# K of batches 2 to 7 by a casting DMA and DMA transposes, in an attention and SwiGLU kernel

## The chip, the core and the metric

One core of a Trainium2 chip runs the whole program. Its engines work side by side, each through its own queue of instructions in order, and wait for each other through semaphores: PE (TensorE; the profile lists its weight loads apart, as PEld), DVE (VectorE), ACT (ScalarE), POOL (GpSimd) and SP (SyncE, which here only issues DMAs). Sixteen DMA engines move data for all queues. The metric is the device time of the program in microseconds (us). Three runs of the kernel before gave 383.66, 384.03 and 384.58 us; their median is 384.03.

## What is computed

Causal attention over 8 batches of 8 heads, 576 tokens and 64 values per head, with a decay from the running sums of `s`, followed by RMS norm and a gated feed-forward network (FFN) over the 8 x 576 = 4608 tokens of width 512:

```python
scores = scale * np.matmul(q, k.transpose(0, 1, 3, 2))
cum = np.cumsum(np.maximum(s, 0.0), axis=-1)
bias = -(cum[:, :, :, None] - cum[:, :, None, :])
scores = np.where(causal, -1000000000.0, scores + np.minimum(bias, 0.0))
attn = np.exp(scores - max); attn = attn / sum
x = matmul(attn, v)                       # heads side by side: 4608 x 512
xn = x / sqrt(mean(x * x) + 1e-6) * rms_g
g = xn @ w_gate; silu = g / (1 + exp(-g))
out = (silu * (xn @ w_val)) @ w_out       # 512 -> 1536 -> 512
```

Inputs and output are float32; the kernel's matmuls run in bfloat16 (bf16). A second, general path in the program is taken only where a test on the data fails; it isn't taken here.

## The kernel before

**Two kinds of work on one queue.** The FFN goes over nine chunks of 512 tokens (`ffn`, L622). For each chunk PE makes twelve pairs of groups of four 128x512 matmuls (L632 for the gate, L641 for the value) and then four output blocks of twelve matmuls (L654). That is 36 groups of four. After each group `step` (L566) is called once: one *slot*. In a slot a scheduler written in the kernel may put a piece of attention of a coming batch behind the FFN group. So the order on every engine is fixed when the program is built; the scheduler counts slots and knows no times. The conditions are written as "so many slots after" (`ready`), and if something is late on the chip, the engine that needs it waits with everything behind it.

**The pieces of attention.** The 576 tokens of a batch are five blocks of 128 (the last of 64). Scores are computed transposed, keys in rows.

- *Loads* (`load_kq`, L122): K and Q of a batch in float32 by DMAs of the ACT queue, four tokens per row, into `kq32`, 1024 KB and a tail of 128 KB each. V (`load_v`, L162) by blocks with DMAs from POOL that cast to bf16, 128 KB each as written.
- *Casts*: POOL casts K (`cast`, L140) and Q (`cast_x`, L148) to bf16 in `kqn`, which has two halves, for even and odd batches; five casts each per batch.
- *Check* (`check_mag`, `check_max`): DVE takes the greatest magnitude of K and of Q.
- *Transposes of Q* (`kq_dma`, L152) for batches 2 to 7 (`XB` is 2): five DMA transposes on SP into `kqTx`, the blocked view of `kqT`, four of them from 32 rows and the last from 64.
- *Transposes of K* for all batches, and of Q for batches 0 and 1: the T step (`t_step`, L169) of a pair of heads makes four PE matmuls against the identity into a PSUM bank, and ACT (for K) copies the result into `kqTn`, the view of `kqT` by heads. A tail step (`tail_step`, L183) does the last 64 tokens with four matmuls for K. The bank has the tag T, which the second AV step of a block uses too (L281).
- *S step* (`s_step`, L214) of batch b, key block kb and half g of the heads, written S(b,kb,g): scores of a key block against its own query block and the next, four matmuls of 64x256 (L236), then eight exps on ACT (L260) and a mask on POOL (L269).
- *AV step* (`av_step`, L278): eight matmuls with V (L286, L292), division on DVE, squares on ACT, then `al_all` on POOL.
- *xnT*: DVE scales the rows (L324), and a DMA transpose on SP (L334) puts them into `xnT`, which the FFN reads.

**Queues.** SP carries, in order, the transposes of Q, those for xnT and the output stores (L661). POOL carries casts, V loads, masks and `al_all`. `x_seq` holds the waiting transposes of Q, which are issued at least two slots apart; `t_seq` the T steps, and `can_t` keeps these two or three slots apart for batches 2 and later; `can_s` (L509) lets an S step go when its Q transposes were issued five slots before and its T steps three. `casts(b + 2)` is queued by the tail step of batch b.

Of the kernel before, what the change touches and what calls it, by code (L numbers as in the profile page):

```python
# [26 lines left out]
def kernel(  # L27
# [12 lines left out]
    nc = tc.nc  # L40
# [6 lines left out]
    NSC = 5  # L47
# [94 lines left out]
    def cast_x(eng, b, w, hp):  # L142
# [6 lines left out]
        else:  # L149
            cast(eng, b, w, 4, 5)  # L150

    def kq_dma(b, w, c):  # L152

        if c < 4:
            src = kqn[32 * c:32 * c + 32, b % 2, w, 0:4].rearrange("p r h d -> p (r h d)")
            dst = kqTx[:, b % 2, w, c].rearrange("d h (r p) -> d (h r) p", r=4)
        else:
            src = kqn[0:64, b % 2, w, 4].rearrange("p h d -> p (h d)")
            dst = kqTx[:, b % 2, w, 4, :, 0:64]
        nc.sync.dma_start_transpose(out=dst, in_=src)  # L160
# [21 lines left out]

    def tail_step(b):  # L183
        pT = psT()
        nw = 2 if b < XB else 1
        for w in range(nw):
            for hp in range(HP):
                i = w * HP + hp
                nc.tensor.matmul(
                    pT[:, i, :], lhsT=kqn[:, b % 2, w, 4, 2 * hp:2 * hp + 2, :],  # L190
                    rhs=ident_bf, is_transpose=True, start=(i == 0), stop=(i == nw * HP - 1))
        dst, src = kqTn[:, b % 2, 0, :, 512:576], pT[:, 0:HP, 0:64]
        if b == 0:
            nc.vector.tensor_copy(out=dst, in_=src)
        else:
            nc.scalar.activation(out=dst, in_=src, func=AF.Copy)
        if nw == 2:
            nc.vector.tensor_copy(out=kqTn[:, b % 2, 1, :, 512:576], in_=pT[:, HP:8, 0:64])
# [15 lines left out]
    def s_step(b, kb, g, pair=None):  # L214

        p = b % 2
        N = (256, 256, 256, 192, 64)[kb]
        W = 64 if kb == 4 else 256
        nj = 4 if kb == 4 else 2
        e = take_slot((b, kb, g), 2 if kb in (0, 1, 2, 3) else 2)  # L220
        if pair is None:
            ps = psS()
            pair = (ps[:, 0, :], ps[:, 1, :])
        heads = []
        for j in range(nj):
            hp = (0 if kb == 4 else 2 * g) + j
            for par in (0, 1):
                rs = slice(par * 64, par * 64 + 64)
                kT = kqTn[rs, p, 0, hp, kb * 128:kb * 128 + 128]
                if b < XB:  # L230
                    qT = kqTn[rs, p, 1, hp, kb * 128:kb * 128 + N]
                    M = N
                else:
                    qT = kqTx[rs, p, 1, kb, hp, 0:64] if kb == 4 else kqTx[rs, p, 1, kb:kb + 2, hp, :]
                    M = W
                nc.tensor.matmul(  # L236
                    pair[par][:, j * W:j * W + M], lhsT=kT, rhs=qT,
                    start=(j == 0), stop=(j == nj - 1))
# [36 lines left out]
        second.mask = mask  # L275
        return second
# [82 lines left out]
    def check_max(i):  # L359
# [12 lines left out]
    s_seq.sort(key=lambda x: (1, 0, x[2], x[1]) if x[0] == 1 and x[1] < 2 else (x[0], x[1], x[2], 0))  # L372
    av_seq = [(b, qb, g) for b in range(B) for qb in range(NSC) for g in (0, 1)]
    xt_seq = [(b, qb) for b in range(B) for qb in range(NSC)]
    t_seq = [(b, hp, w) for b in range(B) for hp in list(range(HP)) + ["tail"]
             for w in (0, 1) if w == 0 or (hp != "tail" and b < XB)]
    t_seq.sort(key=lambda x: (x[0], 9, 0, 0) if x[1] == "tail" else
               (x[0], x[1] // 2, x[2], x[1]) if x[0] == 1 else (x[0], x[2], x[1], 0))
# [4 lines left out]
    def at(*key):  # L383
        return done.get(key, 10 ** 6)

    def ready(lag, *key):
        return at(*key) + lag <= slot[0]
# [13 lines left out]
        t = slot[0] + lag  # L401
        queue.extend((lambda: slot[0] >= t and phase() < 24, f) for f in fns)

    def check(b, ws=(1, 0)):
        dve_side.extend((lambda: (phase() >= 25 if b > 1 else slot[0] % 2
                                  and chunk[0] == b), f) for w in ws for f in (
            lambda w=w: check_mag(b, w), lambda: check_max(0), lambda: check_max(1),
            lambda w=w: done.__setitem__(("check", b, w), slot[0])))

    def phase():  # L410

        return slot[0] - first[0]
# [14 lines left out]
    def casts(b):  # L427


        def over(w):  # L430
            done["cast", b, w] = slot[0]
            if b + 1 < B:
                loads(b + 1, w, early, 4)
            if w == 1:
                x_seq.extend((b, 1, c) for c in range(NSC))
            else:
                done["cast", b] = slot[0]
                check(b)
        fns = [(1, lambda r=r: cast_x(nc.gpsimd, b, 1, r)) for r in range(NSC)]
        fns += [(1, lambda: over(1))]  # L440
        fns += [(0, lambda r=r: cast(nc.gpsimd, b, 0, r, r + 1)) for r in range(NSC)]
        pool_side.extend((lambda w=w: ready(7, "raw", b, w) and ready(0, "check", b - 2, w)
                          and (b < XB + 2 or ready(4, "X", b - 2, 1, 4)), f)
                         for w, f in fns + [(0, lambda: over(0))])

    def after_tail(b):
        if b + 2 < B:
# [49 lines left out]
    def can_t():  # L497
        if not t_seq:
            return False
        b, hp, w = t_seq[0]  # L500
        if b >= XB and at(*(("XT", 1, 3) if b == 2 else ("AV", b - 1, (2, 1, 0, 0, 0)[b - 3], 1))) > slot[0]:
            return False
        if b >= XB and av_seq[0][2] == 1 and can_av(True):
            return False
        if slot[0] - last["T"] < (1 if b < XB else 2 if b < 4 else 3) or slot[0] - last["AVT"] < 3:
            return False
        return (ready(2, "cast", b) or ready(2, "cast", b, w)) and (b < 2 or ready(1, "S", b - 2, 4, 0))

    def can_s():  # L509
        if not s_seq or not slot_free():  # L510
            return False
        b, kb, g = s_seq[0]
        if b == 1 and (phase() < 24 and phase() % 2 == 0 or kb == 4 and at("AV", 1, 3, 1) > slot[0]):
            return False
        due = SLOTS * ((b * S + kb * 128) // DM) - (26 if b == 1 else 18 if b < 4 else 14)
        if slot[0] - last["S"] < (4 if slot[0] < due - 24 else 3 if slot[0] < due else 2):
            return False
        if b >= XB:
            return (all(ready(5, "X", b, 1, c) for c in (kb, min(kb + 1, 4))) and (
                ready(3, "T", b) if kb >= 3 else  # L520
                all(ready(3, "T", b, hp, 0) for hp in (2 * g, 2 * g + 1))))
        if kb >= 3 and not ready(3, "T", b):
            return False
        if kb == 4:
            return True
        return all(ready(3, "T", b, 2 * g + j, w) for j in (0, 1) for w in (0, 1))
# [39 lines left out]
    def step(bare=False):  # L566
# [15 lines left out]
        run_side(act_side)  # L582
        if not moved and x_seq and slot[0] - last["X"] >= 2:
            b, w, c = x_seq[0]
            if ready(2, "cast", b, 1) and ready(1, "S", b - 2, 4, 0):
                x_seq.pop(0)
                kq_dma(b, w, c)
                done["X", b, w, c] = last["X"] = slot[0]
        bare = bare or chunk[0] == 0 and 30 <= phase() <= 33
        if slot[0] % 2 and not bare:  # L590
            run_side(v_side)
# [12 lines left out]
        if can_av():  # L604
            do_av(av_seq.pop(0))
            n += 1
        if n < 2 and can_t():
            do_t(t_seq.pop(0))

    def need(c):  # L610
# [124 lines left out]
    with tc.manual_schedule():  # L735
# [127 lines left out]
            lambda: load_v(1, 3), lambda: load_v(1, 4)])  # L863

        loads(2, 1, later, 14)
        loads(2, 0, later, 18)
        check(0, (0,))
        check(1)
        casts(2)
# [193 lines left out]
```

## Time and profile before

The profiled execution spans 383.2 us from its first to its last instruction; the granted TensorE clock is 0.995 of full speed on average.

| What | us | Where it is read |
|---|---|---|
| median of the runs | 384.03 | the times |
| span of the profiled execution | 383.2 | head of the page |
| PE / DVE / ACT / POOL busy | 349.6 / 286.1 / 247.4 / 172.7 | part 1 of the page |
| first FFN matmul of chunk 0, 1, 2, 8 | 31.5, 76.6, 115.6, 345.0 | weight loads of L632 |
| POOL casts of L140 (of K, and of tails) | 46, 32.6 in all | part 5 |
| V loads, issue on POOL | 40, 35.4 in all | part 5 |
| V load, issue to landing | 3.4 / 4.8 / 19.0 | min, median, max of tile v_sb |
| xnT transpose, issue to landing | 2.9 | median, part 6 of the page by DMA |
| DMA queues' time, of 16 engines | 30.5%, 26.6%, 15.3% | q0 (POOL), q1 (SP), q10 (ACT) |

How to read it: a busy share is an average over the whole span. PE's matmuls overlap in the array, so a matmul's own duration (about 0.38 us for 512 columns) is longer than the distance between two of them (about 0.21 us); what an instruction costs PE's queue is seen from the start of the next group. The time of a DMA's packets contains what they wait for each other, so the shares of the queues can add up to more than the engines have.

### The profile page before, as it was taken

To read this page: it belongs to the slowest core of one execution; us is meant where nothing else is said; L and a number is where in the kernel's file an instruction comes from. 1 tells how busy PE (TensorE), PEld (TensorE's weight loads), DVE (VectorE), ACT (ScalarE), POOL (GpSimd) and SP (SyncE) were. 2 spreads that over 40 slices of the span, in tenths; PEclk is the share of its full clock that TensorE was granted. 3 is DMA by queue.
4 is the path that set the end of the run, shared out by engine and by line. 5 is a ranking of instruction groups with operands and counts; after the bars stand their busy time and mean duration, and the time that the engine had idled before them with its cause. 6 is when DMAs were issued, how large, how long until landed. Compare 5 with 4: busy or idle time off the path is not lost. (4 is left out here: it accounts for less than half of the span.)

```text
span 383.2 us, 7015 instructions
## 1 busy us (share of the span) xinstructions
PE 349.6 (91%) x2391; PEld 165.5 (43%) x2436; DVE 286.1 (75%) x525; ACT 247.4 (65%) x646; POOL 172.7 (45%) x277
## 2 busy tenths in 40 slices
PE   1767999899999999999989999999999999999992
PEld 1443544444444444444434444444444444444441
DVE  6768988499888879987988977984388539837720
ACT  3777787457886687768678757776986774323311
POOL 5866725956774496619734764362223220000000
PEclk9999999999999999999999999999999999999997
DMA  7999999999998896796559083981200221020011
GB/s 232 183 229 232 141 221 179 149 200 196 131 187 214 172 173 98 197 201 51 78 186 225 16 89 92 122 63 42 98 15 9 55 98 21 3 83 28 2 56 60
DMA packets 103292, 46.24 MB, mean 121 GB/s; under 512 B 78481, under 2 KB 98449, under 8 KB 103249
## 3 DMA queue, kind: packets, MB, share of 16 engines
q0 software_dynamic: 41168, 9.44, 30.5%
q1 hardware_dynamic: 43184, 21.97, 26.6%
q10 hardware_dynamic: 18896, 14.30, 15.3%
q8 instruction: 21, 0.34, 0.4%
q14 instruction: 23, 0.18, 0.2%
HBM read 38.16 MB, written 9.44 MB: 124 GB/s over the span
## 5 line engine op out<-in xcount | busy, mean ns | idle before, releaser
L260 ACT ACTIVATE E<-psS,biasK 128x256 bf16<-128x256 f32 (+3 forms) x352 | 114.3, 427 | 8.7 <-PE psS L236 7.6
L641 PE MATMUL psF<-xnT,wv_sb 128*128 128x512 bf16 x417 | 110.0, 380 | 1.0 <-DVE Ht L637 0.2
L632 PE MATMUL psF<-xnT,wg_sb 128*128 128x512 bf16 x419 | 109.1, 379 | 1.8 <-ACT xnT L350 0.7
L654 PE MATMUL psF<-wout_sb,Ht 128*128 128x512 bf16 x416 | 100.8, 379 | 0.8 <-issue 0.2
L269 POOL TENSOR_SCALAR_AFFINE_SELECT E<-E 128x512 bf16<-128x512 bf16 x72 | 52.8, 733 | 94.8 <-ACT E L260 94.1
L635 ACT ACTIVATE T<-psF 128x512 f32<-128x512 f32 x108 | 64.5, 600 | 46.8 <-PE psF L632 40.1
L644 DVE SCALAR_TENSOR_TENSOR U<-T,psF 128x512 bf16<-128x512 f32 x108 | 73.7, 682 | 22.3 <-ACT T L635 22.1
L637 DVE TENSOR_TENSOR Ht<-U,psF 128x512 bf16<-128x512 bf16 x99 | 67.6, 683 | 7.1 <-PE psS L236 0.5
L632 PEld LDWEIGHTS <-wg_sb 128*128 128x128 bf16 x432 | 38.9, 97 | 42.8 <-issue 4.8
L654 PEld LDWEIGHTS <-Ht 128*128 128x128 bf16 x432 | 38.6, 98 | 42.8 <-issue 3.3
L641 PEld LDWEIGHTS <-wv_sb 128*128 128x128 bf16 x432 | 38.1, 98 | 43.0 <-issue 6.4
L324 DVE SCALAR_TENSOR_TENSOR xs_sb<-x_sb,al_all,g_row 128x512 bf16<-128x512 bf16 (+1 forms) x40 | 33.6, 842 | 16.0 <-POOL al_all L317 15.2
L307 ACT ACTIVATE xs_sb<-x_sb 128x512 bf16<-128x512 bf16 (+1 forms) x36 | 22.8, 637 | 32.5 <-DVE x_sb L301 31.8
L659 ACT ACTIVATE osb<-psF 128x512 f32<-128x512 f32 x36 | 21.7, 602 | 28.2 <-PE psF L654 20.2
L164 POOL DMA_DIRECT2D v_sb<-in_v_dram x40 | 35.4, 884 | 0.0
L140 POOL CAST kqn<-kq 128x512 bf16<-128x512 f32 (+1 forms) x46 | 32.6, 728 | 3.9 <-DMA kq<-in_k_dram 3.9
L361 DVE TENSOR_TENSOR acc<-acc,mag 128x1280 bf16<-128x1280 bf16 x32 | 32.4, 1034 | 0.3
L314 POOL TENSOR_SCALAR al_all<-ss_all 128x1 f32<-128x1 f32 (+1 forms) x40 | 10.9, 272 | 45.2 <-ACT xs_sb L307 40.2
L236 PE MATMUL psS<-kqT 64*128 64x256 bf16 (+2 forms) x304 | 26.6, 261 | 3.7 <-ACT E L260 2.5
L292 PEld LDWEIGHTS <-E 128*128 128x128 bf16 x320 | 22.3, 99 | 13.9 <-POOL E L269 3.5
L173 PE MATMUL psT<-ident_bf,kqn 128*128 128x128 bf16 x124 | 13.9, 227 | 12.2 <-ACT kqn L138 8.3
L317 POOL TENSOR_TENSOR al_all<-al_all,mhalf 128x1 f32<-128x1 f32 (+1 forms) x40 | 23.2, 581 | 3.3
(93 smaller groups left out, 288.3 us busy)
## 6 DMA issues: line engine op xcount, KB each, us to landing
out_dram<-osb SPq DMA_DIRECT2D x36, 256.0 KB, 2.2
kq<-in_q_dram ACTq DMA_DIRECT2D x6, 1024.0 KB, 8.5
kq<-in_k_dram ACTq DMA_DIRECT2D x6, 1024.0 KB, 7.7
v_sb<-in_v_dram POOLq DMA_DIRECT2D x32, 128.0 KB, 4.6
wg_sb<-in_moe_w_gate_dram POOLq DMA_DIRECT2D x2, 768.0 KB, 7.3
wv_sb<-in_moe_w_val_dram POOLq DMA_DIRECT2D x2, 768.0 KB, 10.4
wout_sb<-in_moe_w_out_dram POOLq DMA_DIRECT2D x1, 1536.0 KB, 14.4
kq<-in_k_dram SPq DMA_DIRECT2D x2, 512.0 KB, 6.5
```

Of the source, the lines that this page charges most:

```text
L140: eng.tensor_copy(out=o, in_=i)
L164: nc.gpsimd.dma_start(out=v_sb[0:n, b % 2, c, :, 0:64], in_=v[b, :, c * 128:c * 128 + n, :].rearrange("h p d -> p h d"))
L260: nc.scalar.activation(out=eo, in_=ei, func=AF.Exp, scale=0.125, bias=biasK[:, kb, bh:bh + 1])
L269: nc.gpsimd.affine_select(out=Ev[:, :, 0:nq], in_=Ev[:, :, 0:nq], pattern=[[0, nh], [1, nq]], compare_op=ALU.is_ge, fill=0.0, base=0, chan ...
L324: nc.vector.scalar_tensor_tensor(out=xs_sb[0:n, (b * NSC + qb) % NX, :], in0=x_sb[0:n, (b * NSC + qb) % NX, :], scalar=al_all[0:n, col:col ...
L361: nc.vector.tensor_tensor(out=acc[:, sl], in0=acc[:, sl], in1=mag[:, sl], op=ALU.max)
L632: nc.tensor.matmul(Gp, lhsT=wg_sb[:, cc, fs], rhs=xnT[:, cc, x0:x0 + DM], start=(cc == 0), stop=(cc == CC - 1))
L635: nc.scalar.activation(out=T, in_=Gp, func=AF.Tanh, scale=0.5)
L637: nc.vector.tensor_tensor(out=Ht[:, fb - 1, :], in0=pend[0], in1=pend[1], op=ALU.mult)
L641: nc.tensor.matmul(Vp, lhsT=wv_sb[:, cc, fs], rhs=xnT[:, cc, x0:x0 + DM], start=(cc == 0), stop=(cc == CC - 1))
L644: nc.vector.scalar_tensor_tensor(out=U, in0=T, scalar=1.0, in1=Gp, op0=ALU.add, op1=ALU.mult)
L654: nc.tensor.matmul(Op, lhsT=Ht[:, fb, tb * 128:(tb + 1) * 128], rhs=wout_sb[:, fb, :], start=(fb == 0), stop=(fb == FB - 1))
```

## The change

For batches 2 and later K isn't loaded in float32 any more. `load_k` loads it by blocks of 128 tokens with a DMA from POOL that casts to bf16, in the form of `load_v`, straight into `kqn`. `kq_dma` transposes K too, one DMA transpose per block on SP, from 128 rows (64 for the last) into the blocked view, in plain token order. The T steps and tails of batches 2 to 7 are gone, and `s_step` reads K from the blocked view. The five float32 casts of K per batch and the two K loads on ACT's queue are gone as well.

Five rules of the order go with it. `x_seq` holds Q and K transposes in turn; the distance of two slots stays, and K's waits until the load was issued seven slots before. `can_s` asks for the K transpose of the block five slots before, as for Q's. `casts(b + 2)` of batches 2 and later is queued by the last K transpose of batch b in place of the tail step. The K loads wait for the check of K of batch b - 2 and for the readers of that half (T steps, then K transposes). The check takes K first, at least eight slots after its last load was issued.

```diff
+    def load_k(b, c):
+        n = rows(c)
+        nc.gpsimd.dma_start(
+            out=kqn[0:n, b % 2, 0, c],
+            in_=k[b, :, c * 128:c * 128 + n, :].rearrange("h p d -> p h d"))
+
     def kq_dma(b, w, c):
-        if c < 4:
+        if w == 0:
+            n = rows(c)
+            src = kqn[0:n, b % 2, 0, c].rearrange("p h d -> p (h d)")
+            dst = kqTx[:, b % 2, 0, c, :, 0:n]
+        elif c < 4:
             src = kqn[32 * c:32 * c + 32, b % 2, w, 0:4].rearrange("p r h d -> p (r h d)")
...
-                kT = kqTn[rs, p, 0, hp, kb * 128:kb * 128 + 128]
                 if b < XB:
+                    kT = kqTn[rs, p, 0, hp, kb * 128:kb * 128 + 128]
                     qT = kqTn[rs, p, 1, hp, kb * 128:kb * 128 + N]
                     M = N
                 else:
+                    kT = kqTx[rs, p, 0, kb, hp, :]
...
-    t_seq = [(b, hp, w) for b in range(B) for hp in list(range(HP)) + ["tail"]
+    t_seq = [(b, hp, w) for b in range(XB) for hp in list(range(HP)) + ["tail"]
...
-    def check(b, ws=(1, 0)):
-        dve_side.extend((lambda: (phase() >= 25 if b > 1 else slot[0] % 2
+    def check(b, ws=(0, 1)):
+        t = slot[0] + 8
+        dve_side.extend((lambda w=w: (phase() >= 25 and slot[0] >= t and (w == 0 or ready(0, "cast", b, 1))
+                                  if b > 1 else slot[0] % 2
...
+        def key(c):
+            load_k(b, c)
+            done["K", b, c] = slot[0]
+            if c == NSC - 1:
+                check(b)
+
+        def over():
+            done["cast", b, 1] = slot[0]
             if b + 1 < B:
-                loads(b + 1, w, early, 4)
-            if w == 1:
-                x_seq.extend((b, 1, c) for c in range(NSC))
-            else:
-                done["cast", b] = slot[0]
-                check(b)
-        fns = [(1, lambda r=r: cast_x(nc.gpsimd, b, 1, r)) for r in range(NSC)]
-        fns += [(1, lambda: over(1))]
-        fns += [(0, lambda r=r: cast(nc.gpsimd, b, 0, r, r + 1)) for r in range(NSC)]
-        pool_side.extend((lambda w=w: ready(7, "raw", b, w) and ready(0, "check", b - 2, w)
-                          and (b < XB + 2 or ready(4, "X", b - 2, 1, 4)), f)
-                         for w, f in fns + [(0, lambda: over(0))])
+                loads(b + 1, 1, early, 4)
+            x_seq.extend((b, w, c) for c in range(NSC) for w in (1, 0))
+
+        def free():
+            return ready(0, "check", b - 2, 0) and (
+                ready(0, "T", b - 2) if b < XB + 2 else ready(4, "X", b - 2, 0, 4))
+        pool_side.extend((free, lambda c=c: key(c)) for c in range(NSC))
+        fns = [lambda r=r: cast_x(nc.gpsimd, b, 1, r) for r in range(NSC)] + [over]
+        pool_side.extend((lambda: ready(7, "raw", b, 1) and ready(0, "check", b - 2, 1)
+                          and (b < XB + 2 or ready(4, "X", b - 2, 1, 4)), f) for f in fns)
...
         if b >= XB:
-            return (all(ready(5, "X", b, 1, c) for c in (kb, min(kb + 1, 4))) and (
-                ready(3, "T", b) if kb >= 3 else
-                all(ready(3, "T", b, hp, 0) for hp in (2 * g, 2 * g + 1))))
+            return ready(5, "X", b, 0, kb) and all(
+                ready(5, "X", b, 1, c) for c in (kb, min(kb + 1, 4)))
...
-            if ready(2, "cast", b, 1) and ready(1, "S", b - 2, 4, 0):
+            if (ready(2, "cast", b, 1) and ready(1, "S", b - 2, 4, 0)
+                    and (w == 1 or ready(7, "K", b, c))):
                 x_seq.pop(0)
                 kq_dma(b, w, c)
                 done["X", b, w, c] = last["X"] = slot[0]
+                if (w, c) == (0, NSC - 1) and b + 2 < B:
+                    casts(b + 2)
...
         loads(2, 1, later, 14)
-        loads(2, 0, later, 18)
```

In the instruction order of the changed program the attention of batch 2 begins five slots earlier than before (S(2,0,0) in slot 41 in place of 46, counted from the start of chunk 0), that of batch 3 four slots, that of batch 4 nine, and that of batches 5 to 7 twelve to fifteen slots earlier. The last AV step is 13 slots earlier, in chunk 6 in place of chunk 7.

More of the change, by code (lines that the diff above doesn't have):

```diff
@@ L184, in tail_step @@
         pT = psT()
-        nw = 2 if b < XB else 1
+        nw = 2
         for w in range(nw):
@@ L427, in casts @@
     def casts(b):
-        def over(w):
-            done["cast", b, w] = slot[0]
-            if b + 1 < B:
-                loads(b + 1, w, early, 4)
-            if w == 1:
-                x_seq.extend((b, 1, c) for c in range(NSC))
-            else:
-                done["cast", b] = slot[0]
-                check(b)
-        fns = [(1, lambda r=r: cast_x(nc.gpsimd, b, 1, r)) for r in range(NSC)]
-        fns += [(1, lambda: over(1))]
-        fns += [(0, lambda r=r: cast(nc.gpsimd, b, 0, r, r + 1)) for r in range(NSC)]
-        pool_side.extend((lambda w=w: ready(7, "raw", b, w) and ready(0, "check", b - 2, w)
-                          and (b < XB + 2 or ready(4, "X", b - 2, 1, 4)), f)
-                         for w, f in fns + [(0, lambda: over(0))])
+        def key(c):
[5 more added lines that the diff above has]
+            done["cast", b, 1] = slot[0]
+            if b + 1 < B:
+                loads(b + 1, 1, early, 4)
[7 more added lines that the diff above has]
+                          and (b < XB + 2 or ready(4, "X", b - 2, 1, 4)), f) for f in fns)
     def after_tail(b):
@@ L500, in can_t @@
         b, hp, w = t_seq[0]
-        if b >= XB and at(*(("XT", 1, 3) if b == 2 else ("AV", b - 1, (2, 1, 0, 0, 0)[b - 3], 1))) > slot[0]:
+        if slot[0] - last["T"] < 1 or slot[0] - last["AVT"] < 3:
             return False
[L503 to L507, printed above, removed]
+        return ready(2, "cast", b, w)
     def can_s():
@@ L606, in step @@
             n += 1
-        if n < 2 and can_t():
+        if n < 2 and t_seq and can_t():
             do_t(t_seq.pop(0))
```

## The prediction

> **What bounds the kernel now.** I read the page first, then the windows by chunk, then the groups of one line, then the timeline. The page's first two parts:
>
> ```profile
> PE 349.6 (91%) x2391; PEld 165.5 (43%) x2436; DVE 286.1 (75%) x525; ACT 247.4 (65%) x646; POOL 172.7 (45%) x277
> ...
> PE   1767999899999999999989999999999999999992
> ...
> DMA  7999999999998896796559083981200221020011
> ```
>
> TensorE (PE) is busy in nine tenths or more of nearly every slice from the fifth on. The DMA engines are full for the first twelve slices (to about 115 us) and mostly idle after the thirtieth. A window for FFN chunk 2 and one for chunk 8 (which has no attention inside) show what the attention costs:
>
> ```profile
> 115.62:155.18 39.56, 38.23 (x273) 17.94 (x277) 34.25 (x58) 28.83 (x79) 25.67 (x40) 1.00 0.86 156
> ...
> 344.99:383.20 38.21, 31.19 (x142) 14.04 (x145) 17.51 (x31) 9.90 (x18) 0.00 (x0) 0.95 0.10 37
> ```
>
> Columns: span, then busy time of PE, PEld, DVE, ACT, POOL, clock, DMA share, GB/s. The 144 FFN matmuls of a chunk need about 31 us; chunks 1 to 6 take 38.6 to 40.2 us because some 8 us of attention matmuls sit between them on the same queue. PE is the bound, at full granted clock (1.00), so what leaves PE shortens the run, and whatever PE waits for lengthens it.
>
> **What goes from PE.** K of batches 2 to 7 has been transposed by 24 T steps (four matmuls each, L173) and six tails (four each, L189): 120 matmuls. The first row below is that of L173 in the window 76 to 296 us, which holds all 24 T steps; the others are PE's timeline:
>
> ```profile
> L173 PE MATMUL psT<-ident_bf,kqn 128*128 128x128 bf16 x96 | 9.3, 219 | 1.6 <-DVE x_sb L301 1.6
> ...
> 80.34 1.03 PE L632 MATMUL psF<-xnT,wg_sb 128*128 128x512 bf16 x4
> 81.20 0.39 PE L173 MATMUL psT<-ident_bf,kqn 128*128 128x128 bf16 x4
> 81.43 1.03 PE L641 MATMUL psF<-xnT,wv_sb 128*128 128x512 bf16 x4
> ```
>
> The 219 ns are a pipelined latency. The cost to the queue is the delay of the next FFN group: 81.43 - 81.20 = 0.23 us. 30 x 0.23 = 6.8 us. Some T steps also waited for their PSUM bank, which they share with the second AV step of a block: 1.6 us in this row, 3.1 us in the waits of the weight loads for the same steps (PEld L173 <- DVE x_sb); I take 2.3. ACT loses 24 evictions of 0.63 us and six of 0.40, 17 us in all. ACT isn't the bound (28.8 of 39.6 us in chunk 2), so this is worth only what PE waits for ACT at S steps (PE psS <- ACT E, 1.8 us after 72 us): between 0 and 1.8, I take 0.6. **Gain: 6.8 + 2.3 + 0.6 = 9.7 us** (8.4 to 11.7).
>
> **What is added elsewhere.** POOL: 30 casts at 0.727 us go (21.8 us), 30 DMA issues come, at the 0.884 us of the V issues (26.5 us): 4.7 us more, spread over batches, beside PE's work; POOL is busy 26 of 39 us in chunks 1 and 2. Without that cover, the masks (L269) behind an issue would be late, then the AV step that reads them. Each POOL DMA also waits until the eighth before it has landed; ten K and V issues of batch 3 stand within ten slots (11 us), so the last two wait where a block lands later than that, up to 4 us by the slowest landing of that stretch (14.7). ACT's queue loses 12 load issues. DVE's check of K now waits for a DMA landing, with U and Ht queued behind it; the last load of a batch is issued 21 or more slots before it (a slot is a group of four FFN matmuls with what is put behind it, about 1.1 us), more than the 19.0 us of the slowest V landing, so I put it at nothing; what came later would stop U, Ht and then PE for as long. SP: 30 transposes more at 1.2 us of issue, in order with the output stores and xnT transposes. The xnT ones that they now stand before have nine slots or more until their chunk needs them, so I count nothing for these either.
>
> DMA engines: a V block has the form of the new K block (1024 packets). In a quiet window, 172 to 184 us:
>
> ```profile
> q0 software_dynamic: 4170, 0.53, 68.7%
> ```
>
> 68.7% of 12 us for 4170 packets is 2.0 us of all 16 engines per block, so 9 us for K of a batch. The fp32 K load takes 4.9 us (15.3% of 383.2 us over twelve K and Q loads). So 4 us more per batch, with five transposes of the xnT form. From 60 to 110 us the engines are full, and transfers there get later, not only more.
>
> **The new wait.** The S step of a batch now needs the transposed K block besides the transposed Q blocks, all issued on SP alternately, at least two slots apart, and the schedule asks for only five slots between the last needed transpose and the S step. In the instruction order of the changed program, the distance from the last Q transpose to the first S step is 5 slots for batches 2, 3 and 4 (12, 17 and 34 before); for batches 5 to 7 it is 19 or more, so there is no wait there. Everything of PE, the FFN groups too, is queued behind that S step. So the transposes' landing decides:
>
> ```profile
> 75.45 1.23 SPq L160 DMA_TRANSPOSE kqT<-kqn  x1
> 77.28 0.34 SPq L661 DMA_DIRECT2D out_dram<-osb  x1
> 77.70 6.38 SPq L160 DMA_TRANSPOSE kqT<-kqn  x3
> ...
> DMA to landing us min/median/max: 2.7/5.5/10.0
> ```
>
> The last line is that of all 30 Q transposes. The DMA issues of the window 77 to 79 us have the one of 77.70:
>
> ```profile
> kqT<-kqn SPq DMA_TRANSPOSE x1, 9.4
> ```
>
> *Batch 2.* S(2,0,0) stands right behind the fifth FFN group of chunk 1, where now a T step starts at 81.20. It needs Q block 1. K block 0 takes the SP place of the transpose of 75.45, so Q block 1 goes out behind the store of 77.28, at 77.70, as the third Q transpose does now. That one landed after 9.4 us, at 87.1: PE waits 5.9 us. Bounds: the second (75.45) landed after 5.9 us, which leaves 2.4; the slowest after 10.0, 6.5.
>
> *Batch 3.* S(3,0,0) is in the slot that has S(2,4,0) now, at 112.8. Its Q block 1 is behind an xnT transpose that by today's clock is issued at 107.9, so at 109.1. Landing: 2.7 to 10.0 us. Beside V loads alone (233 to 246 us) the median is 3.3, beside K and Q loads (154 to 166) 5.4; here V and K blocks still drain, and no fp32 load: 4.5. PE waits 0.8 (0 to 6.3).
>
> *Batch 4.* S(4,0,0) is in the slot at about 145.8 us. Ahead of its Q block 1 on SP are the two halves of an xnT transpose, whose slot is at 136.5, and K block 0. The xnT transpose of 142.4 was issued 2.5 us behind its slot, so 139.0, and with three issues of 1.2 us 142.6. Landing, with one fp32 load beside it instead of two, between the 3.3 and the 5.4: 4.7. PE waits 147.3 - 145.8 = 1.5 (0 to 6.8).
>
> The second S steps have 7 to 9 slots; for these and for POOL's wait I add 0.5 (0 to 4). **Loss: 5.9 + 0.8 + 1.5 + 0.5 = 8.7 us** (2.4 to 23.6).
>
> Both end on PE's queue, so they add. Against the profiled span of 383.2 us: -9.7 + 8.7 = -1.0. The runs' median, 384.0, is 0.8 above that span, so **383.0 us**; with all bounds -9.3 to +15.2.
>
> [...]
>
> **Rivals.**
> *Faster: the transposes land early.* The K load that competes at 83 to 97 us is gone, and beside V loads alone transposes land in 2.7 to 4.5 us. Then the wait of batch 2 is 2.4, of 3 and 4 nothing: 384.0 - 9.7 + 2.4 + 0.5 = 377.2. Against: at 77.70 that load hadn't begun, and the slow landing was there.
> *Slower: the DMA queues stay full.* 27,648 small packets more (6 x 4608, each 128 bytes) than the 41,168 of today's q0; K and V of batch 3 together are nine blocks, 18 us at best and, at the 74% of 16 engines that 8475 packets took at 60 to 100 us (3.6 us a block), 32 us. If all three transposes take 10.0 us, the waits are 6.5 + 6.3 + 6.8 + 0.5 = 20.1: 384.0 - 9.7 + 20.1 = 394.4. With one landing L for all three the waits are 3 x L - 10.4 + 0.5, which reaches 9.7 at L = 6.5 us; from there on it's slower. For it: 9 to 10 us were usual at 77 to 92 us. Against: 3 to 6 us after 110.
> [...]
> *The change doesn't do what it says:* the built order has 80 transposing matmuls of K and Q left of 200, 30 K issues and 60 transposes; set aside.
>
> **How the numbers follow.** Forecast 0.50, early landing 0.24, full queues 0.21, POOL held 0.05. The forecast's own range is 379 to 387. The whole range, 376.5 to 391.5, takes in the early landing and half of the full queues. A measurement tells about 0.2% (0.8 us) from no change. The forecast's half splits 0.23 faster, 0.11 same, 0.16 slower; with the rivals 0.47, 0.11, 0.42.
>
> **What would show it.** PEld or PE at the S line waiting for DMA kqT, some 6 us near 81 us and under 2 us twice later; nothing after batch 4. No transposing matmul of kqn after 51 us. Chunks 5 and 6 shorter by 1 to 1.5 us for the same attention steps. K issues near 0.9 us. The forecast is wrong if the wait in chunk 1 is under 2 us or above 10, if S steps wait in batches 5 to 7, or if DVE's check or POOL's K issue shows waits for DMA.

## The result and the profile after

Four runs of the changed kernel took 401.68 to 405.33 us, median 403.77; the kernel before took 384.1 beside it. The ratio is 1.0505 (95% interval 1.0471 to 1.0539): slower by 19.7 us, outside the predicted range of 376.5 to 391.5 us. The profiled execution took 403.54 us with a span of 401.9, which is 18.7 us more than the span before; the mean granted clock is 0.962 instead of 0.995. In two experiments below (K loads left out, loads spread) one run each was slower than the others at a lower granted clock; the ratios leave it out, the medians don't.

Parts 1 and 2 of the page after, and three rows of its parts 3 and 5 (q0 is the queue of POOL's DMAs; the S matmuls are L247 now, the K loads L154):

```profile
PE 355.6 (88%) x2316; PEld 161.8 (40%) x2316; DVE 278.9 (69%) x525; ACT 234.3 (58%) x616; POOL 179.1 (45%) x277
...
PE   2787999849998996898599999999999999999991
...
PEclk9999999979998999699699999999999999999996
DMA  8999999997949999669999993690220030020011
...
q0 software_dynamic: 69296, 12.98, 44.2%
...
L247 PE MATMUL psS<-kqT 64*128 64x256 bf16 (+2 forms) x304 | 27.6, 269 | 14.9 <-DMA kqT<-kqn 11.6
...
L154 POOL DMA_DIRECT2D kqn<-in_k_dram x30 | 28.2, 942 | 6.0 <-DMA v_sb<-in_v_dram 6.0
```

ACT lost 13 us of work and PE has fewer matmuls, as meant, yet PE's row, 9 nearly everywhere before, now has four dents between the ninth and the twentieth slice (one slice is 10 us). The clock row has dents at the same places or just behind them. The windows by chunk (columns as before) say where the time is:

```profile
76.31:127.68 51.37, 42.31 (x271) 17.74 (x267) 37.86 (x66) 28.67 (x79) 29.25 (x41) 0.90 1.08 130
127.68:173.06 45.38, 39.81 (x273) 17.58 (x272) 32.91 (x63) 29.59 (x82) 26.99 (x40) 0.92 1.14 154
173.06:220.11 47.05, 40.57 (x262) 17.41 (x261) 32.41 (x61) 28.22 (x77) 28.95 (x41) 0.93 1.34 150
...
257.23:294.28 37.05, 37.05 (x258) 16.64 (x256) 25.69 (x51) 27.14 (x76) 14.01 (x25) 1.00 0.58 83
...
361.90:401.90 40.00, 31.24 (x144) 14.00 (x144) 17.51 (x31) 9.79 (x18) 0.00 (x0) 0.92 0.10 35
```

Chunks 1, 2 and 3 take 51.4, 45.4 and 47.1 us, where chunk 2 took 39.6 before. In chunks 4 to 6 (chunk 5 is shown) PE is busy all the time, and they are 2.5 to 3.1 us shorter than before. The last window, from the first matmul of chunk 8 to the end, has the same PE work as before (31.24 us against 31.19) and is still 1.8 us longer.

Four places make up most of the loss. The timeline shows the first of them, and the fourth with POOL beside it (start, duration, and in brackets the idle time before and what ended it):

```profile
80.04 1.03 PE L648 MATMUL psF<-xnT,wg_sb 128*128 128x512 bf16 x4
87.09 0.61 PE L247 MATMUL psS<-kqT 64*128 64x256 bf16 x4 [6.03 <-DMA kqT<-kqn]
87.63 1.89 PE L657 MATMUL psF<-xnT,wv_sb 128*128 128x512 bf16 x4
89.31 1.91 PE L648 MATMUL psF<-xnT,wg_sb 128*128 128x512 bf16 x4
...
186.82 0.69 POOL L174 DMA_DIRECT2D v_sb<-in_v_dram  x1
193.55 0.68 POOL L154 DMA_DIRECT2D kqn<-in_k_dram  x1 [6.04 <-DMA v_sb<-in_v_dram]
194.24 0.65 POOL L280 TENSOR_SCALAR_AFFINE_SELECT E<-E 128x512 bf16<-128x512 bf16 x1
...
194.95 0.24 PE L303 MATMUL psT<-v_sb,E 128*128 128x65 bf16 x1 [5.25 <-POOL E L280]
```

At 81 us the first S step of batch 2 waits 6.03 us for its transposes. A FFN group of four matmuls takes 1.03 us before the wait and 1.9 us after it: the granted clock is 0.50 from 84.9 to 91.7 us and 1.00 on both sides of that. At 186.8 us POOL has issued V and K loads in one burst and must wait 6.04 us before it may issue the next (the V load issued at 179.06, the eighth before that one, landed after 14.2 us, at 193.3); the mask behind that issue comes late, and the AV step that reads the mask waits 5.25 us. In between, the first S steps of batches 3 and 4 wait:

```profile
122.53 0.61 PE L247 MATMUL psS<-kqT 64*128 64x256 bf16 x4 [2.33 <-ACT xs_sb L318]
...
162.54 0.61 PE L247 MATMUL psS<-kqT 64*128 64x256 bf16 x4 [5.57 <-DMA kqT<-kqn]
```

The first of these two names an ACT instruction that ended at 122.25 us, but the transpose of Q block 1 that the step needs was issued at 118.19 and landed 4.2 us later, at 122.4; that is the later of the two. On SP and in the DMA issues of the windows 118.2 to 118.3 and 155.3 to 155.4 us (the last number is us from issue to landing) the transposes for the two steps are:

```profile
118.19 1.23 SPq L170 DMA_TRANSPOSE kqT<-kqn  x1
...
kqT<-kqn SPq DMA_TRANSPOSE x1, 4.2
...
155.35 1.27 SPq L170 DMA_TRANSPOSE kqT<-kqn  x1
...
kqT<-kqn SPq DMA_TRANSPOSE x1, 7.0
```

A sum of the loss: take the distance between neighbouring FFN matmuls (0.21 us when nothing is between them) and subtract what an S step (0.42) or AV step (0.25) between them takes. The four places then cost 6.3 + 2.6 + 5.9 + 5.6 = 20.4 us. Behind them 10, 7, 8 and 12 FFN matmuls ran at a distance of about 0.43 us, the last of a row partly, which adds 2.0 + 1.4 + 1.8 + 2.8 = 8.0 us. From the start of the last FFN group to the end of the span it is 9.7 us, 7.8 before: 1.9 more. 20.4 + 8.0 + 1.9 = 30.3; the span grew by 18.7, so 11.6 us were gained. This gain is a remainder: whatever the sum leaves out is in it.

### The profile page after: what moved, and what is told of

It is laid out like the page before. It is cut to its first block, busy times and chain, and to the rows that moved or that the text cites. A ratio compares the mean times of both kernels' runs of the same rounds, so it can differ in the third digit from the quotient of the medians.

```text
span 401.9 us, 6880 instructions
## 1 busy us (share of the span) xinstructions
PE 355.6 (88%) x2316; PEld 161.8 (40%) x2316; DVE 278.9 (69%) x525; ACT 234.3 (58%) x616; POOL 179.1 (45%) x277
## 5 line engine op out<-in xcount | busy, mean ns | idle before, releaser
L657 PE MATMUL psF<-xnT,wv_sb 128*128 128x512 bf16 x432 | 114.1, 388 | 0.7 <-DVE Ht L653 0.7
L648 PE MATMUL psF<-xnT,wg_sb 128*128 128x512 bf16 x432 | 112.7, 384 | 0.7 <-ACT xnT L361 0.7
L670 PE MATMUL psF<-wout_sb,Ht 128*128 128x512 bf16 x432 | 104.9, 388 | 0.3 <-DVE Ht L665 0.3
L660 DVE SCALAR_TENSOR_TENSOR U<-T,psF 128x512 bf16<-128x512 f32 x108 | 73.8, 684 | 27.9 <-ACT T L651 27.5
L657 PEld LDWEIGHTS <-wv_sb 128*128 128x128 bf16 x432 | 39.1, 99 | 47.9 <-issue 10.6
L670 PEld LDWEIGHTS <-Ht 128*128 128x128 bf16 x432 | 39.6, 99 | 46.3 <-issue 6.8
L335 DVE SCALAR_TENSOR_TENSOR xs_sb<-x_sb,al_all,g_row 128x512 bf16<-128x512 bf16 (+1 forms) x40 | 31.8, 797 | 16.8 <-POOL al_all L328 15.0
L247 PE MATMUL psS<-kqT 64*128 64x256 bf16 (+2 forms) x304 | 27.6, 269 | 14.9 <-DMA kqT<-kqn 11.6
L154 POOL DMA_DIRECT2D kqn<-in_k_dram x30 | 28.2, 942 | 6.0 <-DMA v_sb<-in_v_dram 6.0
L303 PEld LDWEIGHTS <-E 128*128 128x128 bf16 x320 | 23.0, 101 | 18.6 <-POOL E L280 9.1
L372 DVE TENSOR_TENSOR acc<-acc,mag 128x1280 bf16<-128x1280 bf16 x32 | 28.9, 922 | 0.3
L247 PEld LDWEIGHTS <-kqT 64*128 64x128 bf16 x320 | 10.3, 97 | 43.6 <-issue 36.5
L297 PEld LDWEIGHTS <-E 128*128 128x128 bf16 x256 | 21.4, 102 | 8.3 <-DVE x_sb L312 0.7
```

The lines of the kernel that those rows point to most:

```text
L247: nc.tensor.matmul(pair[par][:, j * W:j * W + M], lhsT=kT, rhs=qT, start=(j == 0), stop=(j == nj - 1))
L335: nc.vector.scalar_tensor_tensor(out=xs_sb[0:n, (b * NSC + qb) % NX, :], in0=x_sb[0:n, (b * NSC + qb) % NX, :], scalar=al_all[0:n, col:col ...
L372: nc.vector.tensor_tensor(out=acc[:, sl], in0=acc[:, sl], in1=mag[:, sl], op=ALU.max)
L648: nc.tensor.matmul(Gp, lhsT=wg_sb[:, cc, fs], rhs=xnT[:, cc, x0:x0 + DM], start=(cc == 0), stop=(cc == CC - 1))
L657: nc.tensor.matmul(Vp, lhsT=wv_sb[:, cc, fs], rhs=xnT[:, cc, x0:x0 + DM], start=(cc == 0), stop=(cc == CC - 1))
L660: nc.vector.scalar_tensor_tensor(out=U, in0=T, scalar=1.0, in1=Gp, op0=ALU.add, op1=ALU.mult)
```

## The experiments

Theory A says that the loss is these four waits, each dearer than its length because the clock falls. The rivals are that a wait costs its length alone (B), that the DMA engines are too full for the change whatever the order (C), and that only the transposes' place on SP counts (D). All times are medians beside runs of the kernel before on the same chip (384.1 to 384.5 us), with the ratio and its 95% interval.

### S steps 12 slots behind their transposes

```diff
-            return ready(5, "X", b, 0, kb) and all(
-                ready(5, "X", b, 1, c) for c in (kb, min(kb + 1, 4)))
+            return ready(12, "X", b, 0, kb) and all(
+                ready(12, "X", b, 1, c) for c in (kb, min(kb + 1, 4)))
```

> S steps of batches 2 to 7 go out 12 slots, not 5, after the transposes they read; nothing else is edited (V loads of batches 4 to 6 move by six to eight slots with the AV steps). Theory A (the loss is four waits of PE, and each costs more than its length because the granted clock is 0.50 for the next eight to twelve FFN matmuls): the three gaps before FFN matmuls near 81, 120 and 157 us (6.95, 3.26, 6.50 us) and their slow matmuls (1.9 + 1.8 + 1.7 us) go, less 0.5 us that an S step takes anyway: 403.8 - 20.6 = 383 us with the AV wait of batch 5 still there, 375 if it goes too. Rival B (a wait costs its length and no more): 403.8 - 15.2 = 388.6. Rival C (the DMA engines are full and the waits only move to a later S, AV or FFN step): above 392.

Measured: 386.33 us, ratio 1.0044 (1.0028 to 1.0059). All three S waits are gone. K(6) and V(5), the loads of K of batch 6 and V of batch 5, mixed in one burst before, are now issued at 171.6 to 177.8 and at 176.6 to 186.7 us, POOL waits 0.3 us for them at most, and the AV wait is gone too. A new wait came at the first group of chunk 2, here in the timeline:

```profile
116.10 0.19 PE L303 MATMUL psT<-v_sb,E 128*128 128x65 bf16 x1
121.82 1.87 PE L648 MATMUL psF<-xnT,wg_sb 128*128 128x512 bf16 x4 [5.53 <-DMA xnT<-xs_sb]
```

S steps that go later make the AV steps and the last xnT transpose of the chunk later. That transpose was issued at 113.68 us, in the middle of five K loads, and took 8.1 us to land where the median of all 36 in this run is 3.8. So seven slots of slack were not free: they came out of the slack of the next link.

### K loads after the V loads of the batch before

```diff
         def free():
-            return ready(0, "check", b - 2, 0) and (
+            return (b < 5 or ready(2, "V", b - 1)) and ready(0, "check", b - 2, 0) and (
```

> K loads of batches 5 to 7 are issued only after the last V load of the batch before, so K(6) no longer stands in one burst with V(5); S steps keep 5 slots. Theory A: POOL's last K issue no longer waits for the software-DMA semaphore, the masks behind it are in time, and the gap near 189 us (6.04 us) goes with its 12 slow matmuls (2.6 us): 403.8 - 8.1 = 395.7 us; the three S waits stay within 1 us of 6.7, 3.0 and 6.3. Rival B: 403.8 - 5.5 = 398.3. Rival C (POOL is late for its own load of work, or DMA contention makes AV late whatever the order): 402 to 405.

Measured: 400.57 us, ratio 1.0408 (1.0380 to 1.0437). The AV wait of batch 5 is gone as theory A had it, and the S waits stayed (6.3, 2.4, 5.3 us). But a wait of 8.5 us appeared elsewhere, and only two rows of ACT explain it:

```profile
224.65 0.63 ACTq L130 DMA_DIRECT2D kq<-in_q_dram  x1
225.38 0.60 ACT L651 ACTIVATE T<-psF 128x512 f32<-128x512 f32 x1 [10.76 <-DMA kqT<-kqn]
...
226.75 1.87 PE L648 MATMUL psF<-xnT,wg_sb 128*128 128x512 bf16 x4 [8.54 <-DVE U L660]
```

ACT issues the Q loads of the next batch. Its second issue waited until a transpose on SP's queue had landed (at 224.6 us), with the tanh of the FFN behind it, then U on DVE, then PE. The first Q load had moved from 204.2 to 212.1 us, and transposes of batch 6 stood between the two issues. So the order of the K loads matters, and a load issue can stop its engine on another queue's DMAs (ACT was idle for 10.76 us here).

### Both edits

> Both edits: 12 slots for the S steps, and K loads of batches 5 to 7 after the last V load of the batch before. Theory A: no FFN gap over 2 us after 76 us, granted clock back to 0.99, and what is left is the gain of the 24 T steps and six tails: 403.8 - 20.6 - 8.1 = 375.1 us, faster than before by 9 us. Rival B: 403.8 - 15.2 - 5.5 = 383. Rival C: above 388. If the clock recovers and the time is still above 380, the gain of leaving T steps out is smaller than 9.7 us.

Measured: 391.22 us, ratio 1.0191 (1.0140 to 1.0243). Theory A's 375 was missed, and rival C's "above 388" was met in the letter. No wait was left at the four old places: the profile has the xnT wait of the first experiment (5.0 us and 2.4 us of slow matmuls) and a wait of 2.0 us at 173 us, where ACT had stood 2.95 us behind its Q load issue. So waits move when the order is changed in one place; whether they must is what the runs below ask.

### K loads left out

The 30 K loads are not issued (`load_k` returns at once), so the K that batches 2 to 7 use is old data; transposes and order stay.

> The 30 K loads are left out (K of batches 2 to 7 is then transposed from stale data); the transposes, their order on SP and the 5 slots stay. It tells whether the waits come from the K loads in the DMA engines and POOL's queue, or from the transposes' own place on SP. Theory A: the wait of batch 2 (K loads were over long before) stays at 5 to 7 us; those of batches 3 and 4, where K loads of the next batch are in flight, fall to under 1.5 and under 3 us; the AV wait goes, as no K issue stands behind the V issues: about 403.8 - 3 - 5 - 8 = 388 us. Rival D (only the transposes' place on SP and the Q loads matter): batches 3 and 4 wait 3 and 6 us as now, only the AV wait goes: 395.7. Rival C (K loads fill the engines everywhere): all waits go, 376.

Measured: 386.45 us, ratio 1.0063 (1.0046 to 1.0080). The S waits from the view of waits (total, count, longest):

```profile
PE psS L244 <- DMA kqT<-kqn: 7.6, 3, 5.7
```

The wait of batch 2 stays (6.0 us by the distance of the FFN matmuls); at the first S steps of batches 3 and 4 0.8 us each are left (and 1.2 at a later one of batch 3), and the AV wait is gone. The transposes of Q block 1 of batches 3 and 4 stand as shortly before their steps as in the change as made, but land sooner (DMA issues of this run at 116.6 and 151.3 us):

```profile
kqT<-kqn SPq DMA_TRANSPOSE x1, 2.7
...
kqT<-kqn SPq DMA_TRANSPOSE x1, 2.7
```

So batches 3 and 4 wait because K loads of the next batch are in flight beside their transposes: without these loads the transposes land after 2.7 us in place of 4.2 and 7.0, and the waits are 0.8 us in place of 2.3 and 5.6. Batch 2's transpose still takes 9.2 us: the K loads aren't its cause, and this run doesn't tell the place of its transposes from the Q and V loads beside them. Rivals C and D both fall. The end of this run is about as long as before: 8.0 us from the last FFN group.

### The T steps left out of the kernel before

`t_step` and `tail_step` return at once for batches 2 and later, so S reads the K of batches 0 and 1. Nothing else of the kernel before is changed.

> The kernel before, with the 24 T steps and six tails of K of batches 2 to 7 left out (matmuls and evictions; S then reads the K of batches 0 and 1); every other instruction stays. It measures the gain term by itself. The prediction's sum (120 matmuls on PE's queue 6.8, PSUM waits 2.3, ACT relief 0.6): 384.5 - 9.7 = 374.8 us, bounds 372.8 to 376.1. Rival, from chunks 5 to 7 of the changed kernel (2.9, 2.5 and 3.1 us shorter, where the sum gives about 1.6 per batch): the steps cost 2.7 us per batch, 384.5 - 16 = 368.5 us.

Measured: 383.05 us, ratio 0.9973 (0.9958 to 0.9989). Both expectations failed: 120 matmuls and 30 evictions less are worth 1.3 us. (The shorter chunks that the second one names are chunks 4 to 6.) The matmuls are out of PE's queue, but PE's waits behind 72 us grew from 7.0 to 10.7 us, as here:

```profile
193.83 0.63 ACT L311 ACTIVATE xs_sb<-x_sb 128x512 bf16<-128x512 bf16 x1 [2.70 <-DVE x_sb L305]
...
196.94 0.29 PE L240 MATMUL psS<-kqT 64*128 64x64 bf16 x8 [2.13 <-ACT E L264]
```

The S step waits for the exps of the one before it; these stood on ACT behind a square, which waited 2.70 us for DVE. With S and AV steps in their old slots, PE only arrives earlier at the same late links.

### Only the evictions left out

The kernel before again, with the T matmuls kept and their copies on ACT left out (S reads old K).

> The kernel before, with only the evictions of those T steps and tails left out (ACT's 24 x 0.63 and 6 x 0.40 us); the 120 matmuls stay on PE's queue. By the prediction's sum (ACT relief 0.6, and most of the 2.3 of PSUM waits, which end on DVE and AV, stays): 383 to 384 us. Rival: if ACT's evictions delay FFN groups and S steps (tanh and exp queued behind them), the larger part of the gain is here: 379 us or less.

Measured: 384.17 us, ratio 0.9997 (0.9987 to 1.0006), as the sum had it: in the old order ACT's relief alone is worth nothing that could be measured.

### A price for a wait

The kernel before, with 14 casts of 128x512 on POOL ahead of one mask in each of batches 5 to 7:

```diff
...
         def mask():
+            if b >= 5 and (kb, g) == (1, 0):
+                for _ in range(14):
+                    nc.gpsimd.tensor_copy(out=hold_out, in_=hold_in)
```

> The kernel before, with POOL held three times (14 extra casts of 128x512, about 10.2 us) ahead of one mask each of batches 5, 6 and 7, where the granted clock is 1.00 and no DMA is near. It prices a wait of PE by itself. An AV step follows its S step by five slots, which hides about 2.7 us, so PE should wait about 7.5 us three times. Theory A (after a wait the clock is 0.50 for some ten FFN matmuls, each 0.21 us longer): 384.5 + 3 x (7.5 + 2.1) = 413 us, granted clock about 0.97. Rival B (a wait costs its length): 384.5 + 22.5 = 407, clock 0.995. Rival E (the slow clock comes from DMA traffic, not from the wait): also 407.

Measured: 406.51 us, ratio 1.0575 (1.0558 to 1.0593), 22.2 us more. The waits were 8.9, 5.6 and 3.7 us, 18.1 in all (taken as above) and less than expected. The slow work behind them added 2.5, 2.0 and 1.4 us, 6.0 in all from unrounded values; the sum, 24.1, is 1.9 above what the run lost, and B's 18.1 is 4.1 below. Windows around the first wait (the last three numbers are clock, DMA share and GB/s):

```profile
214.00:216.00 2.00, 0.65 (x6) 0.21 (x5) 0.00 (x0) 0.00 (x0) 1.81 (x4) 1.00 0.00 0
...
220.00:222.00 2.00, 0.00 (x0) 0.00 (x0) 2.00 (x1) 0.00 (x0) 1.69 (x3) 0.50 0.00 0
...
226.00:228.00 2.00, 2.00 (x9) 0.99 (x8) 1.90 (x6) 1.52 (x5) 1.46 (x3) 0.50 0.00 0
...
230.00:232.00 2.00, 2.00 (x20) 1.03 (x20) 1.57 (x4) 1.47 (x4) 2.00 (x4) 1.00 1.07 74
```

PE stops at 214.6 us, the clock is at half some 4 us later and stays there for about 5 us after PE has resumed at 223.4, and no DMA runs when it falls. Rival E falls, and B with it. Behind these three waits and the four of the change as made the slow matmuls add 1.4 to 2.8 us each. In the change as made the granted clock is 0.50 from 84.9 to 91.7, 122.4 to 125.9, 160.0 to 166.8 and 194.1 to 200.9 us, the last 3.3 to 6.0 us of each after PE has resumed.

### The order mended, in three versions

First the loads are spread:

```diff
-            return ready(5, "X", b, 0, kb) and all(...)
+            lag = 10 if b == XB else 12
+            return ready(lag, "X", b, 0, kb) and all(...)
...
         def free():
+            if b > 3 and (slot[0] - last["K"] < 3 or slot[0] - last["V"] < 3):
+                return False
...
     def check(b, ws=(0, 1)):
-        t = slot[0] + 8
+        t = slot[0] + 16
...
-        if not moved and x_seq and slot[0] - last["X"] >= 2:
+        if not moved and x_seq and slot[0] - last["X"] >= (1 if x_seq[0][0] == XB and x_seq[0][2] < 2 else 2):
...
```

> The changed kernel with its timing mended: S steps 10 slots (batch 2) and 12 slots (later) behind their transposes, the first four K and Q transposes of batch 2 one slot apart, K loads of batches 4 to 7 at least three slots from each other and from V loads, the check of K 16 slots behind the last load. Theory A (the two waits that the run with both edits still had, at the start of chunk 3's feed near 115 us and near 170 us, came from transposes and loads landing together): no FFN gap over 2 us after 76 us, 374 to 378 us, faster than before by 7 to 10. Rival C (the transposes' traffic itself is too much whatever the order): one or more waits of 3 us and more stay, 382 to 392.

Measured: 381.94 us, ratio 0.9942 (0.9922 to 0.9962): 0.6% faster than before, but not 374 to 378, and the longest wait is 2.3 us, where rival C had 3 and more. Batch 2 still waited:

```profile
86.01 0.40 PE L247 MATMUL psS<-kqT 64*128 64x256 bf16 x4 [2.30 <-DMA kqT<-kqn]
```

The Q load of batch 3 (1024 KB) had been issued beside these transposes, and ACT stood 2.7 us behind another Q load issue near 200 us. The next version moves the Q loads:

```diff
-                loads(b + 1, 1, early, 4)
+                loads(b + 1, 1, early, 16 if b == XB else 1)
...
-            if (ready(2, "cast", b, 1) and ready(1, "S", b - 2, 4, 0)
+            if (ready(6 if b > 3 else 2, "cast", b, 1) and ready(1, "S", b - 2, 4, 0)
...
-        loads(2, 1, later, 14)
+        loads(2, 1, later, 10)
```

with a lag of 14 in place of 10 for batch 2.

> The spread version with the Q load of batch 2 four slots earlier (its transposes then start four slots sooner and S of batch 2 follows the last needed one by 14 slots, at the same slot as in the spread version), the Q load of batch 3 out of the way of batch 2's transposes, and from batch 4 on the Q load ahead of the first transpose. Theory A: the S wait of 2.4 us near 86 us and the U wait of 1.8 us near 204 to 214 us (ACT's Q load issue stood 2.7 us behind the DMA eight before it) go: 381.9 - 4 = 378 us (376 to 380). Rival (waits of S for ACT's exps take their place, as where the T steps alone were left out): 381 to 383.

Measured: 380.77 us, ratio 0.9904 (0.9885 to 0.9924). Both named waits are gone, and no ACT waits took their place beyond 1.1 us, but the earlier transposes of batch 2 stood on SP ahead of the xnT transpose that chunk 1 needs:

```profile
79.07 1.44 PE L651 MATMUL psF<-xnT,wg_sb 128*128 128x512 bf16 x3 [4.31 <-issue]
```

The profile names no releaser; the xnT transpose issued at 73.15 us landed after 5.8 us, at 79.0. With batch 3's Q load moved away, batch 2's transpose of Q block 1 landed after 3.7 us in place of 8.4 in the change as made. That points at this load as the cause of batch 2's wait; since the transposes were issued earlier too, it isn't shown by itself. The last version puts the Q loads of batches 2 and 3 back (14 and 4 slots) and takes 12 slots for every batch.

> As the mended run, but with batch 2's Q load back in its old place (in that run its transposes stood on SP ahead of the xnT transpose that chunk 1 needed, and PE waited 4.3 us near 79 us) and S of batch 2 12 slots behind its transposes; batch 3's Q load in its old place too. Theory A: no wait over 1.5 us after 76 us; 380.8 - 4.3 - 2.0 (slow matmuls after it) + 1 (what remains of batch 2's transposes) = 375.5 us (374 to 378). Rival (waits of S for ACT's exps take the place, as in the two runs without T steps): 379 to 381.

Measured: 375.92 us, ratio 0.9775 (0.9753 to 0.9797): 8.2 us faster than the kernel before and 27.9 faster than the change as made. No wait of PE behind 76 us is over 1.4 us, and the page reads:

```profile
PE 342.8 (91%) x2273; PEld 159.2 (42%) x2316; DVE 277.4 (74%) x525; ACT 234.9 (63%) x616; POOL 176.0 (47%) x277
...
PE   1778899899898999999999999999999999999990
...
DMA  8999999799999599999969936991200220020021
...
q0 software_dynamic: 69296, 12.98, 54.4%
```

The same packets go through q0 as in the change as made, and the DMA row is as full. So rival C is refuted by the best run: the loss doesn't come from the amount of traffic but from where it stands.

### The order freed, without K's DMAs

The kernel before without the T steps (S reads old K), but S and AV steps and loads may follow as in the changed kernel, 12 slots behind Q's transposes; K is still loaded in float32 and cast, and not transposed.

> The kernel before with T steps and tails of batches 2 to 7 left out (as in the run without T steps, S reads old K), and S steps, AV steps and the loads behind them free to follow as they do in the changed kernel (S 12 slots behind Q's transposes); K is still loaded as fp32 and cast by POOL, no K transposes. It tells whether the T steps' time is worth something once the order around them may move. Theory F (the 6.8 us of PE only come out when S and AV steps move away from each other, because S steps wait for ACT's exps and ACT's square waits for DVE): 384.3 - 7 to 10 = 374 to 377 us, waits above 0.25 us under 4 us in all (11 us in the run without T steps). Rival G (something else than PE bounds the attention stages, whatever the order): 382 to 384, as in the run without T steps.

Measured: 379.48 us, ratio 0.9874 (0.9858 to 0.9889), between the two theories. Free order turns 1.3 us into 5.0. PE's waits behind 72 us come to 9.5 us, not under 4 as theory F had it; in the whole run S steps wait 5.2 us for ACT:

```profile
PE psS L236 <- ACT E L260: 5.2, 8, 1.9
```

In the last mended version this row is 2.4 us. What that version has over this one beyond the order (no float32 K loads and casts, other slots for the steps) wasn't taken apart.

## Why the prediction was wrong

The step that failed is the loss: the waits were forecast at 8.7 us, each at its length and with nothing behind it. In its place the runs show 20.4 us of waits, 8.0 us of work at half clock behind them and 1.9 us at the end of the program. Most of the missing waits are batch 4's and POOL's; the clock and the end had no term at all.

**The gain of 9.7 us** was about right in size, by luck, and wrong in its mechanism. (Its first term, 30 x 0.23, is 6.9 and not 6.8.) The remainder of the changed kernel's own sum is 11.6, and the last mended version's last FFN group starts 10.4 us earlier than before's. But the text let the 6.8 us of PE's queue turn into time by themselves because PE was at 91%. Left out alone, the T steps gave 1.3 us: ACT's exps and squares, coupled to the S and AV steps, were hardly behind PE. More of it came out where the S and AV steps could move as well (5.0 us), which the change also allows. The mark that the text gave for it, chunks 5 and 6 shorter by 1 to 1.5 us for the same attention steps, was met by neither: they are 2.5 and 3.1 us shorter. Chunk 5 is so with one S step and one AV step more than before (9 and 10 for 8 and 9), which cost 0.7 us: six T steps and tails are gone from it, some 1.4 us, and most of the rest is idle time of PE, 1.3 us before (39.51 less 38.24) and none after. Chunk 6 has fewer attention steps (6 S and 8 AV for 10 and 11), which alone is 2.4 us.

**Batch 2's wait** was right in kind, 6.03 us against 5.9, and in its closeness lucky: the transpose went out 0.9 us later than forecast (78.58 for 77.70) and landed 1.0 us faster (8.4 for 9.4). **Batch 3's** was 2.3 (0.8; bounds 0 to 6.3): it landed after 4.2 us (4.5 predicted), but SP issued it only 2.0 us before the step's turn instead of 3.7.

**Batch 4's wait** is the first term that was badly mis-sized: 5.6 us for 1.5. The transpose of Q block 1 was issued at 155.35 us, 1.6 us closer to its step than the text had it, and took 7.0 us to land for the 4.7 taken, because K loads of batch 5 were in flight (1.5 + 1.6 + 2.3 is 5.4). With the K loads left out it took 2.7 us and the wait is 0.8.

**POOL's wait** was foreseen in kind (eight DMAs in flight, masks behind) and given 0.5 us with the second S steps, up to 4, at batch 3. It came at batch 5, where K(6) and V(5) are issued together and landed after up to 19.0 us, and cost 5.6. The instruction order showed that burst; the text looked for it in one batch only.

**The price of a wait** was put at nothing without a reason: waits were added at their length. Each of the four was followed by 7 to 12 FFN matmuls at half clock, 8.0 us that neither the sum nor any bound held. From the predicted change of the span to the measured one: -1.0 + 11.7 for the waits (20.4 less 8.7) + 8.0 for the clock + 1.9 at the end of the program - 1.9 for the gain (11.6 less 9.7) = 18.7. The last term closes the sum, so the sum is no proof of it.

**The rivals.** "The DMA queues stay full" (394.4) came nearest in its time. The three transposes took 8.4, 4.2 and 7.0, mean 6.5, which is where its formula turns from faster to slower: it gives 9.2 us for the three S waits, which were 13.9 (6.0, 2.3 and 5.6), since all three transposes went out closer to their steps than it took. It had neither the clock nor the fourth wait. "POOL held" (0.05) was rightly set low: no run shows it. The 30 K issues took 0.94 us each, near the 0.9 that the text looked for, and all the idle time of POOL just before them is the 6.0 us until a V load had landed.

## What to carry to other kernels

Price a wait of PE of several us at its length plus the slow matmuls behind it (1.4 to 2.8 us in the seven cases above), and take that from a place in the trace where PE has stood still. In an order counted in slots, look for each moved transfer's neighbours batch by batch (what else is in flight, what is queued behind its issue on its own engine), and give slack where the next link has some. Work taken from a busy engine may be worth little while the engines just behind it keep their order (1.3 us here, 5.0 with the order freed): leaving the work out alone tells that in one run.

## What was not expected of the hardware

- A wait needn't be long to slow PE, and equal waits cost different amounts. Gaps of 2.6 to 3.3 us between FFN matmuls were followed by 0 to 7 slow ones (none after the 3.0 us of the spread version, seven after 3.0 us in the run with K after V). What decides wasn't tried.
- With K loaded by POOL's DMAs the end of the program is longer: 9.3 to 10.0 us from the start of the last FFN group to the end of the span in the seven kernels with these loads, 7.4 to 8.0 in the six without (before 7.8, K loads left out 8.0, order freed 7.6). The difference lies behind the landing of the last output store: from there to the end it is 4.5 to 5.2 us with the loads and 2.7 to 3.0 without. Why wasn't tried.
- In the run with POOL held, a scaling on DVE of 64x512 took 3.33 us, while POOL ran casts and a mask back to back; of the eight of this form in the kernel before, six took 0.74 us and the others 1.05 and 1.41:

```profile
218.90 3.33 DVE L330 SCALAR_TENSOR_TENSOR xs_sb<-x_sb,al_all,g_row 64x512 bf16<-64x512 bf16 x1 [7.03 <-POOL al_all L323]
```
